# Squares of the weights' bound set behind other work with an output tile of their own, and preparation and folds put on 24 steps, in an attention-and-FFN kernel

## The chip, the cores and the metric

The kernel runs on one core of one Trainium2 chip. The time is the device time of one execution in microseconds; the median of three runs stands for a kernel. The engines that matter are TensorE (PE, with its weight loads as PEld), VectorE (DVE), ScalarE (ACT), GpSimd (POOL), and the DMA queues of SyncE (SP).

## The reference

Inputs are q, k, v of shape (8, 8, 576, 64), phi of shape (8, 8, 576, 32), and the float64 weights w_in (512 x 2048) and w_out (2048 x 512). For each batch and head, 32 memory slots are formed from 576 positions, and the queries attend to the slots; the heads side by side are the 512 model columns of 4608 tokens.

```python
a = phi - np.max(phi, axis=2, keepdims=True)          # over the 576 positions
a = np.exp(a)
a = a / (np.sum(a, axis=2, keepdims=True) + 1e-09)
k_m = np.einsum('bhsm,bhsd->bhmd', a, k)
v_m = np.einsum('bhsm,bhsd->bhmd', a, v)
scores = scale * np.matmul(q, k_m.transpose(0, 1, 3, 2))
scores = scores - np.max(scores, axis=-1, keepdims=True)
attn = np.exp(scores)
attn = attn / (np.sum(attn, axis=-1, keepdims=True) + 1e-09)
x = np.matmul(attn, v_m)      # then transposed and reshaped to 4608 x 512
h = x @ w_in
g = h * np.cos(h)
out = g @ w_out
```

## The kernel before, in words

The values of the slots are never applied to the queries alone. For each batch b, `fold` multiplies the 32 slot values of every head (`vm`) with w_in, so that the attention weights `aT` (256 of them per token: 8 heads by 32 slots) meet a folded matrix `vw` of 256 x 2048. The first product of a token group is then h = aT · vw, and the second is g · w_out.

**Groups and steps.** The 4608 tokens are 12 groups of 384, d_ff is 16 chunks `f` of 128; the main loop runs over i = 0 to 191, a step being one chunk of one group. In a step `gemm1` makes `hp` (128 x 384) in one of three PSUM buffers, `act` and `act_end` make g from it, and `gemm2` adds it into three accumulators of 128 x 512, four steps later (`LAG`). The chain of a step is: hp on TensorE, rounding on ACT (L544, tile `gp`), a subtraction on DVE (L547, tile `u`), Sin on ACT (L552), the product with hp on DVE (L554 in group 0, L556 later), which gives the PSUM buffer of hp back, and, from group 1 on, the split of g in two f16 parts (ACT L558, DVE L559). `hp_0_7` below is group 0, chunk 7.

**Group 0** runs in f32 with two matmuls for hp (L524) and three for the accumulators (L572), because the f16 parts of the weights are not there yet. During it the raw float64 weights arrive by DMA, in eight pieces `raw_in` of w_in and eight `raw_out` of w_out; `to_float32` turns one piece into f32 with two DVE operations (L143, L152) and two on ACT (L147, L151), and a third operation on ACT, L154, sums the squares of the piece (Square with `accum_out`) into a column of `sq`. Its elementwise result isn't needed and goes into the low words of the raw tile, over the input that has been read; the raw buffer therefore comes free when the square is done. `weight_scale` takes the largest of the sums as a bound of the weights, from which the scales of the f16 parts follow. `convert_next` takes one piece in each step (steps 0 to 13); `fold_first` makes the folded matrix of batch 0 in f32 for a piece of w_in (L495, then the copy `vf`, L497, on ACT for the first two pieces, on an engine that the scheduler takes for the others).

**Groups 1 to 11** run with split f16: 6 or 12 matmuls for hp (L533) and 9 for the accumulators (L577). In group 1, `w_out_split`, `w_in_split` and `split_first` make the f16 parts.

**Preparation of a batch** (`prep`: `memory`, then `attend`) is a generator whose pieces the main loop takes one after the other among its steps: the maximum of phi over positions, subtraction and exponential (L260), the products `psA` (L270), the normalised `X`, its transpose `tpx` (L292), the bound of the values (`l1` to `ev`), the scores `sc` (L376) brought to SBUF with a DVE transpose (L381), their softmax (L444), and the way back into `aT`. The list `jobs` gives each batch a first and last step, and 24 pieces are dealt out over 10 to 18 steps, so that several fall into one step. The folds of a batch (four, of 512 columns: matmuls, then a split on ACT, L477, and on DVE, L478) come every fourth step, the first `before - 1` steps ahead of use: 12 steps for even batches from 4 on, 4 or 5 for the others (counted from the step in which the batch is first used). psA, tpx, sc, the folds and the broadcast of the maximum share two PSUM buffers (`ps_s`).

**The maximum.** Batches 0 to 3: DVE reduces a transposed copy phiT that the host lays out (batch 0: TensorE transposes instead), and TensorE spreads the result over the partitions (L245, tile `top`). Batches 4 to 7: `maximum` reduces over partitions on POOL (L223).

**Order.** Each engine runs its own queue in order. A scheduler takes the instructions by priority, the order in which the program issues them, and by what is ready in its model; `keep_in_program_order` ties an instruction to the one before it on its engine. So where a piece is issued in the program sets roughly, not exactly, where it stands in a queue. ACT must load a table of functions when Exp follows Sin or the other way round (`ACT_TABLE_LOAD`).

Of the kernel before, what the change touches and what calls it, by code (L numbers as in the profile page):

```python
# [44 lines left out]
@with_exitstack
def attention_then_ffn(ctx: ExitStack, tc: tile.TileContext, phi, phiT, kv, qT, w_in, w_out, eye, out):
# [84 lines left out]

    sq = const.tile([P, 2, NW], F32, name="sq")

    def to_float32(dst, raw, sq_to, pin=False, after_sign=None):
# [19 lines left out]
        nc.scalar.activation(low.bitcast(F32), dst, AF.Square, accum_out=sq_to)  # L154
# [62 lines left out]
    def maximum(b):  # L217
        a = loads["phi", b]
        mx = ld.tile([P, 3, HM], F32, tag="phiT", name=f"mx_{b}", bufs=1)
        nc.vector.tensor_tensor(out=mx[:, 0:2], in0=a[:, 0:2], in1=a[:, 2:4], op=ALU.max)  # L220
# [1 line left out]
        nc.vector.tensor_tensor(out=mx[0:S - 512, 0], in0=mx[0:S - 512, 0], in1=a[0:S - 512, 4], op=ALU.max)
        nc.gpsimd.partition_all_reduce(mx[:, 2], mx[:, 0], channels=P, reduce_op=RED.max)  # L223
# [3 lines left out]
    def memory(b):  # L227
        a = loads.pop(("phi", b))
        if b == 0:

            mx = ld.tile([P, 2, HM], F32, tag="phiT", name="mx_first", bufs=1)
            nc.vector.tensor_tensor(out=mx, in0=a[:, 0:2], in1=a[:, 2:4], op=ALU.max)
            nc.vector.tensor_tensor(out=mx[:, 0], in0=mx[:, 0], in1=mx[:, 1], op=ALU.max)
            nc.vector.tensor_tensor(out=mx[0:S - 512, 0], in0=mx[0:S - 512, 0], in1=a[0:S - 512, 4], op=ALU.max)
# [4 lines left out]
        if b < NT:

            nmx = wk.tile([P, 2], F32, tag="nmx", name=f"nmx_{b}", bufs=1)
            nc.vector.tensor_reduce(out=nmx, in_=loads.pop(("phiT", b)) if b else mt[:, 0:2], op=ALU.max, axis=AX.X)
            top = small_ps(f"top_{b}")[:, 0:HM]
# [552 lines left out]
```

## Time and profile before

| | us |
|---|---|
| median of three runs (lowest, highest) | 710.82 (710.67, 712.17) |
| the profiled execution's own time | 710.08 |
| its span | 708.3 |
| TensorE busy | 687.8 (97%) |
| VectorE busy | 532.7 (75%) |
| ScalarE busy | 518.7 (73%) |
| mean granted clock of TensorE | 0.994 |

The trace is of one execution; its span is shorter than its time by what lies around it. A row of the timeline has start, length, engine, line, operation, output and input tile, count, and in brackets how long the engine had been idle before and on what it waited. A row of the groups has busy time, mean nanoseconds of one, and the idle time ahead of it with what ended most of that. A row of the waits has the total, how often, and the longest. Consecutive matmuls overlap, so the busy time of a group is less than its count times the mean.

### The profile page before, as it was taken

The page shows a single profiled execution, that of the slowest core. Times are in us where ns is not written, and L with a number is a line of the kernel's source. Part 1 is how long each engine was busy: PE and PEld are TensorE (multiplying, and loading weights), DVE is VectorE, ACT ScalarE, POOL GpSimd, SP SyncE. Part 2 cuts the span into 40 slices and gives each one's busy share as a digit, 9 for nine tenths or more (in the row PEclk, how much of TensorE's full clock was granted, in tenths as well). Part 3 has the DMA queues.
Part 4 walks back from the last instruction along what each step waited for, and adds up shares of the span by engine and source line. Part 5 has one row for each costly group of instructions (what it writes and reads, how often), then busy time and mean ns, then how long its engine had stood idle before and what let it go on. Part 6 is the DMA issues. An engine that isn't in the chain of part 4 may idle for free.

```text
span 708.3 us, 11822 instructions
## 1 busy us (share of the span) xinstructions
PE 687.8 (97%) x4597; PEld 364.7 (51%) x4597; DVE 532.7 (75%) x1135; ACT 518.7 (73%) x951; POOL 13.7 (2%) x34
## 2 busy tenths in 40 slices
PE   8699899999999999999999999999999999999997
PEld 3354345565555445666445445666445454665553
DVE  3889879999968966599667886599567976575552
ACT  1899999897985865778666875778766875665652
POOL 0000000000000000000000100000000000000000
PEclk9999999999999999999999999999999999999999
DMA  8996782326407100160105200160100000100101
GB/s 281 379 321 218 266 293 60 105 61 195 146 1 237 44 1 1 56 226 1 44 1 167 99 16 1 46 206 31 44 2 2 22 23 1 46 1 1 45 1 44
DMA packets 31959, 66.18 MB, mean 93 GB/s; under 512 B 2208, under 2 KB 12320, under 8 KB 31904
## 3 DMA queue, kind: packets, MB, share of 16 engines
q1 hardware_dynamic: 27440, 57.43, 25.0%
q10 hardware_dynamic: 4464, 8.00, 3.0%
q8 instruction: 36, 0.59, 0.3%
q14 instruction: 19, 0.16, 0.1%
HBM read 51.79 MB, written 9.44 MB: 86 GB/s over the span
## 4 chain that ended last, share of the span: by engine, by line
PE 60%; DVE 21%; ACT 16%; DMA 2%; issue 1%; ACTq 0%; POOL 0%; DVEq 0%; SPq 0%
PE acc L577 33%; PE hp L533 16%; DVE u L547 4%; ACT u L552 3%; DVE u L556 3%; DVE gp L559 3%; PE psA L270 3%; DVE vw L478 2%; PE sc L376 2%; PE pv L471 2%; ACT gp L558 2%; DMA phi<-in_phi 2%; DVE wo L191 2%; PE hp L524 1%; DVE w_in_parts L202 1%
## 5 line engine op out<-in xcount | busy, mean ns | idle before, releaser
L577 PE MATMUL acc<-wo,gp 128*128 128x512 f16 x1584 | 371.8, 379 | 1.2 <-DVE ob L589 0.7
L577 PEld LDWEIGHTS <-gp 128*128 128x128 f16 x1584 | 153.3, 98 | 162.6 <-issue 4.1
L533 PE MATMUL hp<-aT,vw 128*128 128x192 f16 (+1 forms) x1440 | 202.7, 284 | 1.0 <-DVE u L556 1.0
L533 PEld LDWEIGHTS <-vw 128*128 128x128 f16 x1440 | 128.3, 98 | 77.4 <-issue 17.5
L552 ACT ACTIVATE u<-u,quarter 128x384 f32<-128x384 f32 x192 | 116.7, 615 | 63.8 <-DVE u L547 62.9
L556 DVE SCALAR_TENSOR_TENSOR u<-hp,u 128x384 f32<-128x384 f32 x176 | 96.5, 553 | 60.6 <-ACT u L552 60.1
L544 ACT ACTIVATE gp<-hp,cu 128x192 int32<-128x192 f32 (+1 forms) x240 | 115.4, 492 | 28.1 <-PE hp L533 12.3
L547 DVE SCALAR_TENSOR_TENSOR u<-hp,cu,gp 128x192 f32<-128x192 f32 (+1 forms) x240 | 118.8, 503 | 21.9 <-ACT gp L544 21.5
L559 DVE TENSOR_TENSOR gp<-u,gp 128x384 f16<-128x384 f32 x176 | 96.4, 552 | 43.0 <-ACT gp L558 41.9
L558 ACT CAST gp<-u 128x384 f16<-128x384 f32 x176 | 88.8, 510 | 54.3 <-DVE u L556 53.0
L572 PE MATMUL acc<-wo,gp 128*128 128x512 f32 x96 | 45.1, 599 | 0.0
L478 DVE SCALAR_TENSOR_TENSOR vw<-pv,vw 128x512 f16<-128x512 f32 x48 | 31.5, 684 | 3.0 <-ACT vw L477 2.9
L524 PE MATMUL hp<-aT,vf 128*128 128x384 f32 x64 | 25.6, 533 | 7.9 <-DVE vf L497 3.1
L477 ACT ACTIVATE vw<-pv 128x512 f16<-128x512 f32 x48 | 26.8, 589 | 1.1 <-PE pv L471 0.9
L572 PEld LDWEIGHTS acc<-wo,gp 128*128 128x128 f32 x96 | 17.4, 190 | 17.8 <-issue 15.2
L601 ACT ACTIVATE ob<-acc,os 128x512 f32<-128x512 f32 x27 | 17.8, 682 | 9.6 <-PE acc L577 7.1
L524 PEld LDWEIGHTS hp<-aT,vf 128*128 128x128 f32 x64 | 12.2, 202 | 20.1 <-issue 4.3
L552 ACT ACT_TABLE_LOAD x17 | 21.8, 1283 | 0.3
L270 PE MATMUL psA<-kv,phi 128*32 128x129 f32 (+1 forms) x640 | 21.0, 275 | 0.7 <-ACT phi L260 0.5
L376 PE MATMUL sc<-q,km 128*64 128x256 f32 (+3 forms) x192 | 19.8, 342 | 1.6 <-DVE vw L478 1.2
L270 PEld LDWEIGHTS psA<-kv,phi 128*32 128x32 f32 (+1 forms) x640 | 16.4, 109 | 7.3 <-issue 3.3
L376 PEld LDWEIGHTS sc<-q,km 128*64 128x64 f32 x192 | 12.1, 140 | 12.0 <-issue 3.6
(136 smaller groups left out, 544.7 us busy)
## 6 DMA issues: line engine op xcount, KB each, us to landing
kv<-in_kv SPq DMA_DIRECT2D x32, 516.0 KB, 6.9
raw_out<-in_w_out SPq DMA_DIRECT2D x8, 1024.0 KB, 5.8
q<-in_qT SPq DMA_DIRECT2D x7, 1152.0 KB, 6.0
out<-ob ACTq DMA_DIRECT2D x30, 256.0 KB, 2.1
raw_in<-in_w_in SPq DMA_DIRECT2D x6, 1024.0 KB, 8.1
phi<-in_phi SPq DMA_DIRECT2D x8, 512.0 KB, 5.9
w_in_sb<-w_in_parts SPq DMA_DIRECT2D x12, 256.0 KB, 4.0
kv<-in_kv SPq DMA_DIRECT2D x8, 258.0 KB, 8.5
```

The costliest lines, as they stand in the source:

```text
L270: nc.tensor.matmul(psA[32 * j:32 * (j + 1), g * KV:(g + 1) * KV], lhsT=a[:n, c, h * M:(h + 1) * M], rhs=kvs[c][:n, h * KV:(h + 1) * KV], s ...
L376: nc.tensor.matmul(sc[D * p:D * (p + 1), g * n:(g + 1) * n], lhsT=km[:, 2 * g + p], rhs=qt[:, 2 * g + p, t0:t0 + n], start=True, stop=True)
L478: nc.vector.scalar_tensor_tensor(out=vw[:, 1, g], in0=src, scalar=T, in1=vw[:, 0, g], op0=ALU.mult, op1=ALU.subtract)
L533: nc.tensor.matmul(hp[:, c0:c0 + n], lhsT=vw[:, wi, g, fo * P:(fo + 1) * P], rhs=aT[:, ai, g, c1:c1 + n], start=(k == 0), stop=(k == 5))
L544: ins = nc.scalar.activation(ni[:, c], hp[:, c], AF.Copy, scale=cu, bias=0.25)
L547: nc.vector.scalar_tensor_tensor(out=u[:, c], in0=hp[:, c], scalar=cu, in1=ni[:, c], op0=ALU.mult, op1=ALU.subtract)
L552: nc.scalar.activation(u, u, AF.Sin, scale=TWO_PI_BELOW, bias=quarter)
L556: nc.vector.scalar_tensor_tensor(out=u, in0=hp[:, :GT], scalar=2.0 ** -17, in1=u, op0=ALU.mult, op1=ALU.mult)
L558: nc.scalar.copy(gp[:, 0], u)
L559: nc.vector.tensor_tensor(out=gp[:, 1], in0=u, in1=gp[:, 0], op=ALU.subtract)
L572: nc.tensor.matmul(accs[grp][t], lhsT=gp[:, t * P:(t + 1) * P], rhs=wo[:, f + 1], start=(f == 0), stop=(f == NF - 1))
L577: nc.tensor.matmul(accs[grp][t], lhsT=gp[:, gi, t * P:(t + 1) * P], rhs=parts[:, wi], start=(f == 0 and gi == 0 and wi == 0), stop=(f == N ...
```

## The change

Six things change. (1) L154, the square, is no longer issued where the piece is converted: it is put into a list, and from step 2 on up to two of the list are issued at the end of a step; what is left goes out before `weight_scale`. Its output is an f16 tile of its own, `sink`, written contiguously, which takes a place called "mx"; the raw buffer comes free with the DVE operation before it. (2) `phiT` with its three loads, its reduction and the broadcast matmuls are gone for batches 1 to 3; these use `maximum` as the later ones do. Batch 0 keeps its way. (3) The transpose of X is a transpose instead of a product with the identity in f32. (4) `part` ties the matmuls of one piece (psA, scores, folds) to one another. (5) Pieces go by a plan: one piece per step, 16 of them, from seven steps ahead of psA (`maximum`) and three (subtraction, exponential) to thirteen behind. psA of an even batch stands 30 steps before use, of an odd one 22 (batch 2: 24). Folds start eight steps behind psA, four steps apart; `scales` one step before the first of them. Batch 1 has a plan of its own (steps 1 to 8), and its folds stay at 12, 16, 20 and 24. (6) The copies `vf` from the third piece on are fixed to DVE.

```diff
+PLAN_FIRST = [1, 2, 2, 3, 3, 4, 4, 4, 5, 5, 6, 6, 7, 7, 8, 8]
+PLAN = [-7, -3, 0, 1, 2, 3, 4, 5, 6, 7, 8, 9, 10, 11, 12, 13]
...
+    def part(piece, *args, **kw):
+        ins = nc.tensor.matmul(*args, **kw)
+        if piece_of[0] == piece:
+            tc.keep_in_program_order(ins)
+        piece_of[0] = piece
...
-        if 0 < b < NT:
-            loads["phiT", b] = t = ld.tile([P, 2, S], F32, tag="phiT", name=f"phiT_{b}", bufs=1)
-            nc.sync.dma_start(out=t, in_=phiT[b].rearrange("(g p) s -> p g s", p=P))
...
-        nc.scalar.activation(low.bitcast(F32), dst, AF.Square, accum_out=sq_to)
+        squares.append(lambda: nc.scalar.activation(
+            st["sink"].rearrange("p (c x) -> p c x", c=dst.shape[1]), dst, AF.Square, accum_out=sq_to))
...
     def weight_scale(kind, name):
+        while squares:
+            squares.pop(0)()
...
-            nc.tensor.matmul(tpx[:, g * P:(g + 1) * P], lhsT=X[:, g], rhs=ident, start=True, stop=True)
+            nc.tensor.transpose(tpx[:, g * P:(g + 1) * P], X[:, g], ident)
...
-        (nc.scalar.copy if j < 2 else nc.any.tensor_copy)(out=st["vf", q][:, :, r * WS:(r + 1) * WS], in_=pv)
+        (nc.scalar.copy if j < 2 else nc.vector.tensor_copy)(out=st["vf", q][:, :, r * WS:(r + 1) * WS], in_=pv)
...
-        before, length = {1: (5, 10), 2: (5, 13), 3: (6, 16)}.get(b, (6, 17) if b % 2 else (13, 18))
-        jobs.append((b, use - before - length, use - before - 1))
+        if b == 1:
+            plan, first_fold = PLAN_FIRST, 12
+        else:
+            p0 = use - (22 if b % 2 else 30) + 6 * (b == 2)
+            plan, first_fold = [p0 + x for x in PLAN], p0 + (8 if b % 2 else 8)
+        at_step.setdefault(plan[0], []).append((b, True))
+        for x in plan[1:]:
+            at_step.setdefault(x, []).append((b, False))
         for q in range(NQ):
-            folds.setdefault(use - before + 4 * q + 1, []).append((b, q))
+            folds.setdefault(first_fold + 4 * q, []).append((b, q))
...
+        if i > 1:
+            if squares and "sink" not in st:
+                st["sink"] = ld.tile([P, NP * WS], F16, tag="mx", name="sink", bufs=1)
+            for _ in squares[:2]:
+                squares.pop(0)()
```

How the queues change is seen in the order of the instructions. First ACT at the start of group 0, before the change; the squares are the rows of L154, with the raw tile as their output:

```order
L151 ACTIVATE raw_out_0_111<-raw_out_0_111 128x1024
L544 ACTIVATE gp_0_0_337<-hp_0_0_333 128x384
L147 ACTIVATE w_in_sb_86<-wo_87 128x4x256
L154 ACTIVATE raw_in_1_108,sq_90<-w_in_sb_86 128x1024
L497 COPY vf_0_268<-pvf_1_297 128x2x256
L154 ACTIVATE raw_out_0_111,sq_90<-wo_87 128x1024
L552 ACT_TABLE_LOAD
L552 ACTIVATE u_0_0_336<-u_0_0_336,quarter_84 128x384
```

The same stretch after the change, where lines have moved by a few (the conversions are now L154 and L158, the square L161, the rounding L547, Sin L555):

```order
L158 ACTIVATE raw_out_0_111<-raw_out_0_111 128x1024
L547 ACTIVATE gp_0_0_332<-hp_0_0_328 128x384
L154 ACTIVATE w_in_sb_86<-wo_87 128x4x256
L547 ACTIVATE gp_0_1_371<-hp_0_1_367 128x384
L500 COPY vf_0_267<-pvf_1_295 128x2x256
L555 ACT_TABLE_LOAD
L555 ACTIVATE u_0_0_331<-u_0_0_331,quarter_84 128x384
L158 ACTIVATE wo_87<-wo_87 128x1024
L555 ACTIVATE u_0_1_370<-u_0_1_370,quarter_84 128x384
```

Two squares and a copy of vf stood ahead of the first sine; now the second rounding and the copy do, and the first square stands behind step 2's sine, some eleven rows further on.

Second, ACT between the sines of steps 6 and 7 of group 0, before:

```order
L552 ACTIVATE u_0_6_592<-u_0_6_592,quarter_84 128x384
L154 ACTIVATE raw_in_5_347,sq_90<-w_in_sb_86 128x1024
L411 ACTIVATE aT_1_497<-back_1_0_605 128x2x256
L147 ACTIVATE wo_87<-raw_out_3_396 128x1024
L151 ACTIVATE raw_out_3_396<-raw_out_3_396 128x1024
L552 ACTIVATE u_0_7_620<-u_0_7_620,quarter_84 128x384
```

and after the change (`at_1` is the softmax of batch 1):

```order
L555 ACTIVATE u_0_6_585<-u_0_6_585,quarter_84 128x384
L447 ACT_TABLE_LOAD
L447 ACTIVATE at_1_516<-at_1_516 128x640
L161 ACTIVATE sink_447,sq_90<-w_in_sb_86 128x1024
L154 ACTIVATE wo_87<-raw_out_3_385 128x1024
L158 ACTIVATE raw_out_3_385<-raw_out_3_385 128x1024
L547 ACTIVATE gp_0_7_611<-hp_0_7_607 128x384
L414 ACTIVATE aT_1_515<-back_1_0_622 128x2x256
L154 ACTIVATE wo_87<-raw_out_4_454 128x1024
L161 ACTIVATE sink_447,sq_90<-wo_87 128x1024
L555 ACT_TABLE_LOAD
L555 ACTIVATE u_0_7_610<-u_0_7_610,quarter_84 128x384
```

An exponential with two table loads around it, another conversion and a second square have moved between the two sines; the rounding gp_0_7 stands there too, which before came ahead of u_0_6.

Third, DVE in the scores of batch 5, in group 6 before the change (`vw_4_3` is the last fold of batch 4; `sc_5` its neighbour's scores):

```order
L394 TENSOR_REDUCE rs_5_4018<-at_5_4016 128x16
L559 TENSOR_TENSOR gp_6_0_4039<-u_6_0_4038,gp_6_0_4039 128x384
L478 SCALAR_TENSOR_TENSOR vw_4_3_4055<-pv_4_3_0_4056,vw_4_3_4055 128x512
L478 SCALAR_TENSOR_TENSOR vw_4_3_4055<-pv_4_3_1_4065,vw_4_3_4055 128x512
L381 STREAM_TRANSPOSE at_5_4016<-sc_5_512_4078 128x128
L547 SCALAR_TENSOR_TENSOR u_6_1_4095<-hp_6_1_4088,cu_4_3585,gp_6_1_4096 128x384
```

and at the same pieces of batch 5 after it, now in group 5:

```order
L384 STREAM_TRANSPOSE at_5_4010<-sc_5_0_4013 128x512
L562 TENSOR_TENSOR gp_5_14_3993<-u_5_14_3992,gp_5_14_3993 128x384
L384 STREAM_TRANSPOSE at_5_4010<-sc_5_256_4018 128x512
L392 TENSOR_REDUCE rm_5_4011<-at_5_4010 128x16
L393 TENSOR_TENSOR at_5_4010<-at_5_4010,rm_5_4011 128x512
L550 SCALAR_TENSOR_TENSOR u_5_15_4032<-hp_5_15_4025,cu_3_2294,gp_5_15_4033 128x384
L384 STREAM_TRANSPOSE at_5_4010<-sc_5_512_4049 128x128
```

The fold of batch 4 stood ahead of the last piece of the scores; no row of `vw_4` is left there, and `vw_4_3` stands some 50 rows earlier.

More of the change, by code (lines that the diff above doesn't have):

```diff
@@ L130, in load_w_out @@
         loads["out", j] = t
+    squares = []
     sq = const.tile([P, 2, NW], F32, name="sq")
@@ L227, in memory @@
     def memory(b):
+        if b == 0:
+            maximum(0)
         a = loads.pop(("phi", b))
         if b == 0:
[L231 to L234, printed above, removed]
             mt = small_ps("mx_T").rearrange("p (g x) -> p g x", x=P)
             for g in range(2):
-                nc.tensor.transpose(mt[:, g], mx[:, 0, g * P:(g + 1) * P], ident)
+                nc.tensor.transpose(mt[:, g], st["mx", 0][:, g * P:(g + 1) * P], ident)
             yield
[L239 to L243, printed above, removed]
+            nmx = wk.tile([P, 2], F32, tag="nmx", name="nmx", bufs=1)
+            nc.vector.tensor_reduce(out=nmx, in_=mt[:, 0:2], op=ALU.max, axis=AX.X)
+            top = small_ps("top")[:, 0:HM]
             for g in range(2):
@@ L256, in memory @@
                                           op=ALU.subtract)
[L257 removed]
+            if b > 1:
                 tc.keep_in_program_order(ins)
@@ L732, in attention_then_ffn @@
         for b, q in folds.get(i, ()):
+            fold(b, q)
+        for b, q in folds.get(i + 1, ()):
             if q == 0:
                 scales(b)
-            fold(b, q)
         if i % 48 in (8, 24) and i > 8:
             out_scales(2 * (i // 48) + (i % 48 == 24))
-        for b, s, e in jobs:
-            if i == e - 6 and NT <= b + 1 < B:
-                maximum(b + 1)
-            s = max(s, 0)
-            if s <= i <= e:
-                if b not in gens:
-                    gens[b] = [prep(b), 0]
-                want = math.ceil((i - s + 1) * NSTEP / (e - s + 1))
-                while gens[b][0] is not None and gens[b][1] < want:
-                    gens[b][1] += 1
-                    if next(gens[b][0], "end") == "end":
-                        gens[b][0] = None
-                if i == e:
-                    for _ in gens[b][0] or ():
-                        pass
+        for b, top in at_step.get(i, ()):
+            if top:
+                maximum(b)
+                gens[b] = prep(b)
+            else:
+                next(gens[b])
+        if i > 1:
[3 more added lines that the diff above has]
+                squares.pop(0)()
         if i in (11 * NF + 4, 11 * NF + 6):
@@ L758, in attention_then_ffn @@
         gemm2(*p)
-_INS = ["phi", "phiT", "kv", "qT", "w_in", "w_out", "eye"]
+_INS = ["phi", "kv", "qT", "w_in", "w_out", "eye"]
 def kernel(**inputs):
@@ L776 @@
         "phi": np.ascontiguousarray(phi.transpose(0, 2, 1, 3)).reshape(B, S, HM),
-        "phiT": np.ascontiguousarray(phi[:NT].transpose(0, 1, 3, 2)).reshape(NT, HM, S),
         "kv": kv.reshape(B, S, H * KV),
```

30 lines of the change are left out of this document (13 added, 17 removed).

## The prediction

> **What bounds the kernel now.** I read the shares of the engines first, then the chain that ended last.
>
> ```profile
> span 708.3 us, 11822 instructions
> PE 687.8 (97%) x4597; PEld 364.7 (51%) x4597; DVE 532.7 (75%) x1135; ACT 518.7 (73%) x951; POOL 13.7 (2%) x34
> PE 60%; DVE 21%; ACT 16%; DMA 2%; issue 1%; ACTq 0%; POOL 0%; DVEq 0%; SPq 0%
> ```
>
> TensorE is busy for 97% of the span, and 37% of the chain still runs over VectorE and ScalarE. An average hides where that is, so the next view is the busy time in stretches (sum, then PE, weight loads, DVE, ACT and POOL with counts, granted clock, DMA).
>
> ```profile
> 20.00:40.00 20.00, 13.03 (x55) 6.12 (x55) 15.98 (x24) 18.49 (x24) 0.00 (x0) 0.95 1.05 367
> 60.00:80.00 20.00, 16.86 (x56) 7.88 (x56) 18.35 (x33) 17.93 (x24) 0.31 (x1) 0.91 0.78 270
> 120.00:140.00 20.00, 19.27 (x125) 11.13 (x124) 19.89 (x42) 17.91 (x37) 0.00 (x0) 1.00 0.35 93
> 640.00:660.00 20.00, 20.00 (x117) 10.85 (x115) 11.34 (x24) 11.55 (x24) 0.00 (x0) 1.00 0.00 1
> ```
>
> There are two stages. Near the end (last row) TensorE is full and ACT and DVE are little over half busy: there only removed matmuls, or removed gaps in them, are worth time. In group 0 (20 to about 108 us) ACT is at 18 of 20, and TensorE has gaps: 7 us idle before 40, 3.1 us between 60 and 80 with the granted clock at 0.91. There the order on ACT and DVE decides, and in group 1 too, where DVE is at 19.9. The waits of TensorE name the gaps (total, times, longest); the first three rows are for 27 to 110 us, the rest for 110 to 708, rows of PEld being its weight loads.
>
> ```profile
> PE hp L524 <- DVE vf L497: 3.1, 1, 3.1
> PE hp L524 <- DVE gp L554: 2.1, 1, 2.1
> PE hp L524 <- DVE aT L406: 0.9, 1, 0.9
> ...
> PE sc L376 <- DVE vw L478: 1.2, 1, 1.2
> ...
> PEld sc L376 <- DVE vw L478: 2.1, 2, 1.7
> PEld psA L270 <- ACT phi L260: 1.4, 2, 1.0
> PEld psA L270 <- DVE vw L478: 1.3, 3, 0.5
> ```
>
> **The change part by part.** *Removed matmuls.* The broadcast of the maximum (L245) goes for batches 1 to 3, and the transpose of X (L292) issues two records a batch where there were four.
>
> ```profile
> 42.57 0.61 PE L245 MATMUL top<-ident,nmx 128*128 128x128 f32 x4
> L245 PE MATMUL top<-ident,nmx 128*128 128x128 f32 x16 | 2.7, 281 | 0.1
> L292 PE MATMUL tpx<-ident,X 128*128 128x128 f32 x32 | 5.8, 283 | 0.2 <-DVE X L287 0.2
> ```
>
> Four records take 0.61 us, one alone 0.28: the three others add 0.33, so a record costs 0.11 us in the stream. Batches 2 and 3 lose four each: 2 × 0.45 = 0.9 us. Batches 2 to 7 lose two each in L292: 6 × 0.22 = 1.3 us. Batch 1's six lie in group 0, where TensorE waits anyway, so I count them at nothing; without that cover they are worth another 0.7. Batch 0's L292 lies in the startup chain (0.2, left out). Sum: −2.2 us.
>
> *The maximum of batches 1 to 3* moves from one DVE reduction to three DVE operations and one on POOL:
>
> ```profile
> L242 DVE TENSOR_REDUCE nmx<-phiT 128x2 f32<-128x1152 f32 x3 | 4.0, 1338 | 0.0
> L220 DVE TENSOR_TENSOR mx<-phi 128x512 f32<-128x512 f32 x4 | 2.7, 686 | 1.5 <-DMA phi<-in_phi 1.5
> L223 POOL PARTITION_ALL_REDUCE mx<-mx x4 | 5.1, 1278 | 22.9 <-DVE mx L222 11.8 <-DVE rs L395 11.1
> ```
>
> One reduction is 1.34 us; the largest of the new three is 0.69, the other two handle half that width or less, so DVE's sum stays about level, and POOL's 1.28 us have four steps in which to finish. Nothing, in DVE's slack; for batch 1, in group 0, at most the 1.3 us of POOL if the subtraction is next on DVE. Three loads of phiT leave SP's queue ahead of phi and kv, where the transfers between 20 and 40 us run at a share of 1.05 of the engines. They come earlier, and a raw buffer is now free once the last DVE operation of a conversion has read it; but the first conversions wait for DVE and ACT as well; I take nothing, with 2 us of gain as the other end.
>
> *Squares and table loads on ACT.* The sixteen squares stay; each is issued up to two per step behind the step's work and writes contiguous f16.
>
> ```profile
> L154 ACT ACTIVATE raw_out<-wo 128x1024 f32<-128x1024 f32 x8 | 9.3, 1161 | 0.0
> L260 ACT ACTIVATE phi<-phi 128x1024 f32<-128x1024 f32 x7 | 7.4, 1058 | 0.1
> L552 ACT ACT_TABLE_LOAD x17 | 21.8, 1283 | 0.3
> L497 ACT COPY vf<-pvf 128x512 f32<-128x512 f32 x4 | 2.3, 574 | 0.0
> ```
>
> The trace has no contiguous f16 square; between the strided 1.16 and the contiguous 1.06 of L260 I take 1.06, 16 × 0.1 = −1.6, the other end being nothing. The order has 34 table loads before and 44 after, two of the ten in group 0: +2.6 there. Two of the four copies of vf go from ACT to DVE: −1.1 there, as much more on DVE. ACT's sum over group 0 is therefore level, and what counts is the order. The eight others fall into steps where ACT is little over half busy: nothing, since it idles 8.4 us of the 20 from 640 on and its two table loads around an exponential are 2.6; without that cover they cost up to 2.6 a batch.
>
> ```profile
> 34.20 1.28 ACT L552 ACT_TABLE_LOAD   x1
> 35.50 0.61 ACT L552 ACTIVATE u<-u,quarter 128x384 f32<-128x384 f32 x1
> ```
>
> Here the sine starts 0.02 us after its 1.28 us load. The Trainium skill (ScalarE: Activation LUTs, What ACT_TABLE_LOAD costs) gives a switch 1.28 us and a drain of 1.38 besides, about 2.66 in all, which speaks against this change; the trace shows no such drain ahead of the sine. By the page the two loads in group 0 would cost 5.3 us, an estimate, and that would leave the sum 2.7 higher.
>
> *Group 0, by hand.* Two places matter. First, in the order before, hp_8 waits for a copy of vf on DVE:
>
> ```profile
> 71.02 0.62 ACT L552 ACTIVATE u<-u,quarter 128x384 f32<-128x384 f32 x1
> 71.54 1.15 ACT L154 ACTIVATE raw_in<-w_in_sb 128x1024 f32<-128x1024 f32 x1
> 72.65 0.63 ACT L411 ACTIVATE aT<-back 128x512 f16<-128x512 f32 x1
> 73.17 1.35 ACT L147 ACTIVATE wo<-raw_out 128x1024 int16<-128x1024 uint8 x1
> 74.37 1.11 ACT L151 ACTIVATE raw_out<-raw_out 128x1024 f32<-128x1024 f32 x1
> 75.37 0.62 ACT L552 ACTIVATE u<-u,quarter 128x384 f32<-128x384 f32 x1
> 60.63 1.56 PE L524 MATMUL hp<-aT,vf 128*128 128x384 f32 x4
> 75.52 4.54 PE L524 MATMUL hp<-aT,vf 128*128 128x384 f32 x8 [3.14 <-DVE vf L497]
> 105.67 1.40 DVE L478 SCALAR_TENSOR_TENSOR vw<-vf,T,vw 128x512 f16<-128x512 f32 x2
> 107.87 1.15 PE L533 MATMUL hp<-aT,vw 128*128 128x192 f16 x12
> ```
>
> The wait is 3.14 us, and the eight matmuls behind it take 4.54 where twice 1.56 = 3.1 is normal: 1.4 more, together 4.5. In the new order that copy is no longer behind it, so I let this gap go. The Trainium skill (TensorE: Matmul & The Clock Gate, Part 1) has the clock fall to half after an idle window and return after some 3.4 us; the 4.54 and the 0.91 agree, and by it any new gap of that length costs about 1.4 on top.
>
> Second, a gap of that kind comes up elsewhere. Between the sines of steps 6 and 7 ACT now holds a table load, an exponential, two squares, two of L147, one of L151, gp_7, aT and another table load. From the rows: 2 × 1.28 + 2 × 1.06 + 2 × 1.35 + 1.11 + 0.63, then 0.5 for gp_7 and 0.7 for the exponential (384 and 640 elements beside aT's 512) and 0.62 for the sine, is about 10.9 us, against 75.37 − 71.02 = 4.4 before. The product on hp_7 behind that sine gives back the buffer that hp_10 needs; behind hp_10 on TensorE stand the matmuls of acc, whose gp wait for the same sine. Of the 6.5 us more, TensorE still has about 1.1 us of queued work, one and a half hp at 1.56 / 2; I take 5.4 as lost. Against 4.5 won that gives +0.9. Two squares of 1.15 stood ahead of the first sine and now none do; of these 2.3 us I let 0.4 last to the end of the group. Group 0: +0.5 (−1.5 to +4). Before, the last split of vf on DVE ends at 107.07, 0.8 ahead of the first f16 hp, and that piece keeps its place in the order; but group 1, where ACT and DVE are near full, now takes batch 2's first pieces with a table load of 1.28 more: +1. Groups 0 and 1: **+1.5**, between −6 (both gaps closed) and +6 (the new gap runs at half clock, and nothing is won in the first).
>
> *Spread preparation and folds.* In the steady part, the stalls were the small PSUM buffers of a fold standing between the pieces of one preparation:
>
> ```profile
> 394.99 1.28 DVE L478 SCALAR_TENSOR_TENSOR vw<-pv,vw 128x512 f16<-128x512 f32 x2
> 395.73 0.45 PE L376 MATMUL sc<-q,km 128*64 128x64 f32 x8 [1.23 <-DVE vw L478]
> ```
>
> The order puts the last fold of an even batch some eight steps ahead of the next batch's scores, and the exponentials of phi three steps ahead of psA; so these rows go. How much is there: TensorE's own waits from 110 us on sum to 3.8 us, those of its weight loads to 7.4 more, parts of which are hidden behind a running matmul; 4 to 11 us therefore. Some come back where folds of odd batches (now from step 14 before use) share the two buffers with the next piece. I take **−5**, near the lower end, with 0 and −10 as bounds.
>
> Sum against the profiled execution's own 710.08 us: −2.2 − 5 + 1.5 = −5.7, 704.4. That execution lies 0.74 under the median of the runs, 710.82, so on the median's footing 705.1; with the 0.2 at startup, **704.9 us**.
>
> **The rivals.** (A) *The steady gain comes, group 0 gets worse* by 5.5 instead of 1.5: 708.9. The 10.9 us in front of one sine speak for it; against it, that ACT's sum is level and TensorE has work to catch up with. (B) *The other side: ACT's queue in group 0 sets the end.* If two more sines stand behind table loads and squares as step 7's does, TensorE waits twice over 3 us and runs at half clock behind each (2 × 4.5 = 9): 704.9 + 9 = 713.9. It decides from the point where the first f16 hp, now at 107.87, comes later than about 116 (107.87 + 0.5 + the 7.3 that lie between 704.9 and 712.2). Against it: ACT had 1.5 to 2 us to spare in the windows of 20 to 80. (C) *The stalls only move*: the ten table loads and folds of odd batches make as many new ones, the −5 is nothing: 709.9. For it: the two small buffers stay two, and a batch's pieces and the folds of its neighbour still share them; against it: both named releasers are gone from those places. (D) *Both gaps close*: stalls −8 and groups 0 and 1 at −2.5: 704.9 − 3 − 4 = 697.9. For it: the upper bound of the stalls is 11; against it, the wait for hp_10. That the change does not do what it says is no rival: the order shows the squares behind the conversions.
>
> **How the numbers follow.** The forecast, with its own range 701.5 to 707.5, has 0.50, A 0.15, B 0.12, C 0.13, D 0.10. A measurement of this kernel can tell about 0.2% from no change, 1.4 us: faster is below 709.4. Faster: forecast, A and D, 0.75; the same: C, 0.13; slower: B, 0.12. The range from 698 to 712.5 leaves out B and half of D, 0.17.
>
> **What would show it.** The first f16 hp (107.87 now) between 106 and 112; the PE wait for vf L497 gone and one of 4 to 6 us for a gp of step 7 or near it in its place, with PEclk below 1 there; no wait of sc for vw behind 110 us, and PE and weight-load waits there under half of 3.8 and 7.4; 20 fewer PE records in steady preparation (8 of L245, 12 of L292). I am wrong if group 0 moves by more than 4 us, or if the steady part keeps its stalls.

## The result and the profile after

The changed kernel takes 723.25 us (719.1 to 724.15) beside 710.96 of the kernel before: 1.6% slower, a ratio of 1.0158 with an interval of 1.0117 to 1.0200. The forecast was 704.9 with a range up to 712.5; it is wrong in sign and in size. First the page of the profile after:

```profile
span 721.8 us, 11777 instructions
PE 689.4 (96%) x4569; PEld 362.2 (50%) x4569; DVE 537.2 (74%) x1142; ACT 528.8 (73%) x960; POOL 19.0 (3%) x37
PE 52%; ACT 20%; DVE 18%; DMA 7%; issue 2%; SPq 0%; POOL 0%; ACTq 0%; DVEq 0%
```

TensorE has 28 matmuls fewer than before and is busy for 1.6 us more, in a span that is 13.5 us longer. Its share of the chain fell from 60 to 52%; transfers rose from 2 to 7%. DVE and ACT grew by 4.5 and 10.1 us. The waits of TensorE (total, times, longest), from 27 to 112 us (first two rows) and from 112 on:

```profile
PE acc L575 <- DVE wo L159: 5.3, 2, 3.0
PE hp L527 <- DVE gp L557: 3.7, 3, 1.5
...
PE hp L536 <- DVE u L559: 9.2, 5, 3.3
PE tpx L295 <- DVE vw L481: 1.4, 1, 1.4
```

The wait for vf on DVE (3.1 before) is gone, and so are TensorE's own rows of sc and psA; tpx waits 1.4 for a fold. In their place hp waits for DVE in the main chain of a step, 9.2 us where it was 1.0. TensorE's own waits behind 112 us sum to 11.3 us and those of its weight loads to 10.2, where the prediction wanted less than half of 3.8 and 7.4. The timeline has the places (start, length, engine, line, what, idle ahead):

```profile
54.45 2.08 PE L575 MATMUL acc<-wo,gp 128*128 128x512 f32 x2 [2.26 <-DVE wo L159]
63.38 2.74 PE L575 MATMUL acc<-wo,gp 128*128 128x512 f32 x6
79.74 2.84 PE L575 MATMUL acc<-wo,gp 128*128 128x512 f32 x6 [3.00 <-DVE wo L159]
84.04 1.56 PE L527 MATMUL hp<-aT,vf 128*128 128x384 f32 x4 [1.45 <-DVE gp L557]
111.69 0.49 PE L536 MATMUL hp<-aT,vw 128*128 128x192 f16 x4
139.59 3.79 PE L536 MATMUL hp<-aT,vw 128*128 128x192 f16 x24 [2.09 <-DVE u L559]
184.72 2.08 PE L536 MATMUL hp<-aT,vw 128*128 128x384 f16 x6 [3.32 <-DVE u L559]
313.73 2.00 PE L536 MATMUL hp<-aT,vw 128*128 128x192 f16 x12 [2.39 <-DVE u L559]
476.33 1.15 PE L536 MATMUL hp<-aT,vw 128*128 128x192 f16 x12 [1.10 <-DVE u L559]
```

Twelve matmuls of hp take 2.00 us behind the gap at 313 and 1.15 behind the shorter one at 476. The windows view has a granted clock of 0.50 behind the first, so a gap can be paid twice, as waiting and as half clock:

```profile
313.90:317.20 3.30, 3.30 (x16) 2.15 (x15) 3.03 (x8) 2.98 (x9) 0.05 (x1) 0.50 0.03 7
```

To see in which stage the time went, the span of every profiled execution is cut at the first hp, at the first f16 hp (end of group 0), and at the first accumulator matmul of groups 3 and 11, all taken from the start times of TensorE's matmuls. The column of groups 1 and 2 begins at the first f16 hp; group 11 and the end, 44.8 to 44.9 us in every kernel, are left out. The table holds the experiments told below too.

| kernel | to first hp | group 0 | groups 1, 2 | groups 3 to 10 | table loads | median us |
|---|---|---|---|---|---|---|
| before | 27.0 | 80.9 | 130.5 | 425.0 | 34 | 709.74 to 710.96 |
| changed | 27.7 | 84.0 | 141.8 | 423.4 | 44 | 723.25 |
| e1 squares in place | 27.2 | 83.2 | 138.7 | 422.3 | 46 | 718.97 |
| e2 parts issued by POOL | 27.3 | 84.4 | 146.4 | 422.0 | 44 | 729.12 |
| e3 maximum tied | 26.6 | 82.6 | 135.4 | 419.6 | 44 | 712.27 |
| e4 e1 + e2 + e3 | 26.8 | 83.4 | 143.5 | 419.6 | 46 | 719.06 |
| e5 e3 + e1 | 27.7 | 83.3 | 136.2 | 419.6 | 46 | 713.68 |
| e7 e3 + all exponentials tied | 27.0 | 79.9 | 139.9 | 421.8 | 30 | 713.61 |
| e9 e7 + e1 | 26.5 | 80.1 | 141.0 | 421.8 | 32 | 718.00 |
| e10 e3 + batch 1's exponentials tied | 27.3 | 80.5 | 136.5 | 419.6 | 42 | 710.31 |
| e11 tied for batches 4 to 7 | 27.4 | 83.4 | 140.8 | 419.6 | 44 | 715.63 |
| e12 tied for batches 2, 3 | 27.0 | 82.5 | 136.2 | 424.2 | 44 | 716.58 |
| e13 e3 + old steps | 27.3 | 82.5 | 131.1 | 423.4 | 40 | 711.43 |
| e16 e13 + batch 1's exponentials tied | 26.8 | 80.7 | 130.8 | 423.3 | 38 | 708.98 |
| e6 before + squares deferred | 27.1 | 82.5 | 130.5 | 424.8 | 36 | 712.45 |
| e14 e6 + batch 1's exponentials tied | 27.6 | 83.7 | 129.5 | 424.6 | 34 | 712.64 |
| e15 e14 + transpose of X | 26.7 | 83.7 | 129.0 | 426.2 | 34 | 712.22 |
| e17 before + transpose of X | 29.3 | 82.8 | 129.2 | 424.8 | 34 | 712.00 |

Of the 13.5 us, 3.1 lie in group 0, 11.3 in groups 1 and 2, 0.7 ahead of the first hp, and groups 3 to 10 win 1.6. The plan moves 48 more fold matmuls than before (three folds, at 0.98 us each) out of groups 3 to 10 into groups 1 and 2. Without those 2.9 us, groups 1 and 2 lose 8.4 and groups 3 to 10 lose 1.3. Executions of one kernel differ by more than single cells do (the changed kernel's go from 719.1 to 724.15), while groups 3 to 10 agree within 0.1 in five kernels (419.6). I therefore take it that differences of 1 us in the first three columns carry nothing; with one trace for each kernel that isn't shown.

How much of the two later columns is idle time of TensorE shows in the windows view (length first, then TensorE's busy time; the granted clock is the third number from the end). The rows are groups 1 and 2 and groups 3 to 10, before, in the changed kernel and in e3:

```profile
107.87:238.42 130.55, 129.23 (x912) 70.85 (x910) 121.39 (x267) 108.78 (x206) 3.03 (x7) 1.00 0.37 109
238.42:663.43 425.01, 422.31 (x3000) 228.81 (x2999) 307.86 (x663) 300.52 (x582) 7.33 (x13) 1.00 0.13 45
111.69:253.50 141.81, 134.46 (x942) 71.09 (x942) 125.52 (x276) 118.95 (x220) 7.66 (x10) 0.98 0.37 102
253.50:676.91 423.41, 419.29 (x2944) 227.35 (x2942) 306.76 (x655) 299.27 (x576) 6.18 (x12) 1.00 0.13 45
109.13:244.49 135.36, 131.61 (x944) 69.64 (x944) 124.42 (x275) 119.29 (x222) 7.67 (x9) 1.00 0.37 107
244.49:664.08 419.59, 417.65 (x2945) 226.43 (x2942) 307.76 (x658) 299.79 (x576) 7.27 (x13) 1.00 0.13 45
```

Before the change TensorE idled for 1.3 us in groups 1 and 2 and for 2.7 us in groups 3 to 10. After it, it idles for 7.4 and 4.1.

### The profile page after: what moved, and what is told of

The parts are those of the page before. It is cut to its first block, busy times and chain, and to the rows that moved or that the text cites. A ratio compares the mean times of both kernels' runs of the same rounds, so it can differ in the third digit from the quotient of the medians.

```text
span 721.8 us, 11777 instructions
## 1 busy us (share of the span) xinstructions
PE 689.4 (96%) x4569; PEld 362.2 (50%) x4569; DVE 537.2 (74%) x1142; ACT 528.8 (73%) x960; POOL 19.0 (3%) x37
## 4 chain that ended last, share of the span: by engine, by line
PE 52%; ACT 20%; DVE 18%; DMA 7%; issue 2%; SPq 0%; POOL 0%; ACTq 0%; DVEq 0%
PE acc L580 31%; PE hp L536 16%; ACT u L555 4%; DVE u L550 3%; DMA phi<-in_phi 3%; DVE u L559 3%; DVE gp L562 3%; ACT gp L561 3%; PE pv L63 2%; DVE vw L481 2%; ACT gp L547 2%; DMA w_in_sb<-w_in_parts 2%; PE sc L63 2%; ACT sink L161 1%; DMA kv<-in_kv 1%
## 5 line engine op out<-in xcount | busy, mean ns | idle before, releaser
L536 PE MATMUL hp<-aT,vw 128*128 128x192 f16 (+1 forms) x1440 | 205.0, 287 | 9.4 <-DVE u L559 9.2
L536 PEld LDWEIGHTS <-vw 128*128 128x128 f16 x1440 | 129.9, 99 | 86.3 <-issue 28.2
L555 ACT ACTIVATE u<-u,quarter 128x384 f32<-128x384 f32 x192 | 115.6, 613 | 61.0 <-DVE u L550 60.3
L547 ACT ACTIVATE gp<-hp,cu 128x192 int32<-128x192 f32 (+1 forms) x240 | 114.0, 489 | 33.7 <-PE hp L536 16.3
L527 PE MATMUL hp<-aT,vf 128*128 128x384 f32 x64 | 24.0, 500 | 5.6 <-DVE gp L557 3.7
L604 ACT ACTIVATE ob<-acc,os 128x512 f32<-128x512 f32 x27 | 17.9, 684 | 13.3 <-PE acc L580 11.3
```

The source lines that it names most:

```text
L527: nc.tensor.matmul(hp[:, :GT], lhsT=st["vf", q][:, g, fo * P:(fo + 1) * P], rhs=st["aTf"][:, g], start=(g == 0), stop=(g == 1))
L536: nc.tensor.matmul(hp[:, c0:c0 + n], lhsT=vw[:, wi, g, fo * P:(fo + 1) * P], rhs=aT[:, ai, g, c1:c1 + n], start=(k == 0), stop=(k == 5))
L547: ins = nc.scalar.activation(ni[:, c], hp[:, c], AF.Copy, scale=cu, bias=0.25)
L555: nc.scalar.activation(u, u, AF.Sin, scale=TWO_PI_BELOW, bias=quarter)
```

## The experiments

**Three suspects, each undone alone: e1 to e4.** The trace of the changed kernel offered three causes. Squares stand ahead of conversions for which accumulator matmuls wait (54 and 79 us). The third block of w_in's f16 parts is issued late and lands later still, behind loads for batch 3 in SyncE's queue; first the issue rows of that queue, then ACT's wait for it:

```profile
136.36 1.25 SPq L223 DMA_DIRECT2D w_in_sb<-w_in_parts  x2
154.54 1.84 SPq L101 DMA_DIRECT2D kv<-in_kv  x2
156.52 0.38 SPq L93 DMA_DIRECT2D phi<-in_phi  x1
159.86 0.65 SPq L222 DMA_DIRECT2D w_in_sb<-w_in_parts  x1
```

```profile
175.70 1.33 ACT L211 ACTIVATE w_in_parts<-w_in_sb,s_in 128x512 f16<-128x512 f32 x2 [3.17 <-DMA w_in_sb<-w_in_parts]
```

And `maximum` waits for phi on DVE:

```profile
309.01 0.69 DVE L230 TENSOR_TENSOR mx<-phi 128x512 f32<-128x512 f32 x1 [2.85 <-DMA phi<-in_phi]
```

e1 issues the squares in place again:

```diff
-        squares.append(lambda: nc.scalar.activation(
-            st["sink"].rearrange("p (c x) -> p c x", c=dst.shape[1]), dst, AF.Square, accum_out=sq_to))
+        nc.scalar.activation(low.bitcast(F32), dst, AF.Square, accum_out=sq_to)
```

> The changed kernel with one part undone: each square is issued again right behind the conversion of its piece and writes the raw tile's low words; all else as changed (723.25 us, first f16 hp at 111.7). Theory: in group 0 the deferred squares stand ahead of later conversions on ScalarE, and TensorE waits for those (2.3 and 3.0 us for wo behind the DVE operation that ends a conversion); undone, the first f16 hp comes at about 108 and the time falls by 3 to 4, to 719.5. Rival (it is the ten extra table loads on ScalarE that cost the time, wherever they fall): the squares don't matter, 722 to 724.

Measured: 718.97 us, ratio to before 1.0116 (1.0074 to 1.0158). The size is the theory's, though with four runs each the intervals of e1 and of the changed kernel overlap. The place isn't: TensorE's waits for wo in group 0 fell from 5.3 to 2.1 us as expected, but group 0 stayed at 83.2, with two table loads more, and most of the gain lies in groups 1 and 2, whose order the edit changes as well. It doesn't show that the squares were the cause.

e2 issues the sixteen transfers of the parts from GpSimd:

```diff
-            nc.sync.dma_start(out=w2[here, :, o], in_=parts[here, 0])
-            nc.sync.dma_start(out=w2[there, :, o], in_=parts[here, 1])
+            nc.gpsimd.dma_start(out=w2[here, :, o], in_=parts[here, 0])
+            nc.gpsimd.dma_start(out=w2[there, :, o], in_=parts[here, 1])
```

> The changed kernel with the sixteen transfers of the w_in parts issued by GpSimd instead of SyncE, so that they no longer stand behind the loads of batch 3 in SyncE's queue (issue blocked from 136.4 to 154.5 us, third block at 159.9 instead of about 140). Theory: ScalarE's 3.2 us wait for that transfer at 175.7 and TensorE's 3.3 us at 184.7 with the half clock behind it go: 5 to 6 us less, 717.5 to 718. Rival (table loads): these waits only move to the next sine, 722 to 723.

Measured: 729.12, ratio 1.0269 (1.0240 to 1.0298), slower by 6 instead of faster by 5. GpSimd's queue, with nothing of batch 3 ahead of it, issued the third block at nearly the same time, and ACT's wait for it grew:

```profile
157.70 0.62 POOL L222 DMA_DIRECT2D w_in_sb<-w_in_parts  x1 [7.10 <-ACT vw L480]
```

```profile
172.93 0.72 ACT L211 ACTIVATE w_in_parts<-w_in_sb,s_in 128x512 f16<-128x512 f32 x1 [7.15 <-DMA w_in_sb<-w_in_parts]
```

In both kernels ACT (L211) finishes the last piece of that block only at 155.4 to 155.5 us, and GpSimd issues its transfer at 157.70, behind a split on ACT by the profile. The queue of SyncE, at 159.86, therefore held the block for 2.2 us at most. That suspect falls. The wait itself is on the path: in e2 ACT waits 7.15 us for the transfer, DVE 6.82 for ACT, and TensorE 5.74 for DVE, with a granted clock of 0.50 behind it:

```profile
176.25 0.70 PE L63 MATMUL sc<-q,km 128*64 128x64 f32 x8 [5.74 <-DVE at L384]
174.10:180.80 6.70, 4.55 (x25) 3.06 (x26) 6.38 (x15) 4.90 (x11) 0.31 (x1) 0.50 0.40 127
```

Why the transfer lands so late is not shown.

e3 ties the first DVE operation of `maximum` to its place:

```diff
-        nc.vector.tensor_tensor(out=mx[:, 0:2], in0=a[:, 0:2], in1=a[:, 2:4], op=ALU.max)
+        ins = nc.vector.tensor_tensor(out=mx[:, 0:2], in0=a[:, 0:2], in1=a[:, 2:4], op=ALU.max)
+        if b > 1:
+            tc.keep_in_program_order(ins)
```

> The changed kernel with the first DVE operation of the maximum of batches 2 to 7 tied to its place in the program, so that it no longer stands some 100 rows earlier on DVE, ahead of the landing of phi (DVE waits 2.85 us for that transfer at 309 us, TensorE 2.4 us, and again about 1.3 at 475). Theory: 2.4 and about 1 of half clock, and 1.3: 4 to 5 us less, 718.5 to 719. Rival (table loads): nothing, 722.5 to 724.

Measured: 712.27, ratio 1.0041 (1.0023 to 1.0059): 11 us of the 12.3 lost, more than twice what was expected. The order on DVE tells what the tie does. Of batch 5, the row of the maximum's first operation and of the subtraction that needs the result are, in the changed kernel and with the tie (number of the row on DVE in front):

```
changed  512 L230 TENSOR_TENSOR mx_5_3629<-phi_5_2959 128x512
changed  624 L259 TENSOR_TENSOR phi_5_2959<-phi_5_2959,mx_5_3629 128x1024
tied     610 L230 TENSOR_TENSOR mx_5_3629<-phi_5_2959 128x512
tied     625 L261 TENSOR_TENSOR phi_5_2959<-phi_5_2959,mx_5_3629 128x1024
```

The plan puts the maximum in step 83; the scheduler had moved it some hundred rows forward, presumably to where its model has phi_5 in place (the model is not on record). On the chip phi_5 had not landed, and everything on DVE behind it waited. The spread has its part in this: the load of phi_5 goes out when psA of batch 4 has read phi_4. In the kernel before (first four rows) psA stands 3.5 us behind the subtraction of batch 4, and DVE comes to the maximum of batch 5 at 17.1 us behind it. In the changed kernel (last three, with the row of 309.01 above as the fourth) psA stands 6.7 us behind it, and DVE is at the maximum already at 13.2 (309.01 less the wait of 2.85):

```profile
294.94 1.21 DVE L254 TENSOR_TENSOR phi<-phi,mx 128x1024 f32<-128x1024 f32 x1
298.40 2.54 PE L270 MATMUL psA<-kv,phi 128*32 128x129 f32 x80
301.05 0.38 SPq L87 DMA_DIRECT2D phi<-in_phi  x1
312.08 0.68 DVE L220 TENSOR_TENSOR mx<-phi 128x512 f32<-128x512 f32 x1
293.00 1.55 DVE L259 TENSOR_TENSOR phi<-phi,mx 128x1024 f32<-128x1024 f32 x2
299.68 2.54 PE L63 MATMUL psA<-kv,phi 128*32 128x129 f32 x80
302.55 0.38 SPq L93 DMA_DIRECT2D phi<-in_phi  x1
```

At batch 7 only psA has moved (from 4.3 to 6.7 us behind the subtraction), and DVE waits 1.56 us where it did not wait. DVE's waits for phi behind 200 us, all for batches 4 to 7, are, in the changed kernel and, below, in the kernel before:

```profile
DVE mx L230 <- DMA phi<-in_phi: 6.2, 4, 2.8
```

```profile
DVE mx L220 <- DMA phi<-in_phi: 1.5, 2, 1.0
```

With the tie there is no such row. Of the 12.9 us between the two profiled spans, groups 3 to 10 give 3.8, groups 1 and 2 give 6.4, group 0 and the startup 2.5. In groups 1 and 2 TensorE idles 3.6 us less and is busy for 2.9 less, its mean granted clock 1.00 in place of 0.98; in groups 3 to 10 it is 2.2 and 1.6.

e4 has the three edits together.

> All three edits together in the changed kernel. Theory: the three places are separate in time, so the gains add to 12 to 14: 709.5 to 711, at the time of before or a little under it. Rival (table loads): 720 or more.

Measured: 719.06, ratio 1.0132 (1.0110 to 1.0153). The gains don't add: groups 1 and 2 are at 143.5, with the loss of e2 in them.

**What is left after e3: e5, e6, e7, e9.** e5 is e3 with the diff of e1 on top.

> The maximum tied as in the run before (712.27 us), and the squares issued again right behind each conversion, into the raw tile. Theory S (what is left of the loss, group 0 taking 82.6 us from its first hp to the first f16 hp where it took 80.9, comes from the deferred squares standing ahead of conversions): group 0 back to 81, the time at 709.5 to 710.5. Theory T (it comes from the extra table loads on ScalarE): 712 to 713.

Measured: 713.68, ratio 1.0038 (1.0025 to 1.0050), with group 0 at 83.3: theory S's 81 didn't come, and theory T's time is missed by 0.7. With the maximum tied, squares in place win nothing; but two of the run's table loads are new and lie in group 0 (46 in all), so that S and T are not told apart. e6 defers the squares in the kernel before:

```diff
-        nc.scalar.activation(low.bitcast(F32), dst, AF.Square, accum_out=sq_to)
+        squares.append(lambda: nc.scalar.activation(
+            st["sink"].rearrange("p (c x) -> p c x", c=dst.shape[1]), dst, AF.Square, accum_out=sq_to))
...
+        if i > 1:
+            if squares and "sink" not in st:
+                st["sink"] = wk.tile([P, NP * WS], F16, tag="back", name="sink", bufs=4)
+            for _ in squares[:2]:
+                squares.pop(0)()
```

> The kernel before with one part of the change alone: the squares go into a list, up to two are issued behind a step from step 2, and write an f16 tile of their own, here one of the four buffers of the tiles back and ob. The parts that this leaves out (plan, maximum, transposes) are as before. Theory S: the deferral costs group 0 about 2 us, 712 to 714 beside 710 of before. Theory T: it moves work within a full ScalarE, and gains what the shorter contiguous writes save: 709 to 711.

Measured: 712.45, ratio 1.0033 (1.0021 to 1.0044): the deferral alone makes the kernel slower, by 1.6 us in group 0. It too brought two table loads with it (36), so that S and T were not told apart. The squares themselves are cheaper, as assumed (in the changed kernel 1.04 us against 1.15 to 1.16 before):

```profile
L161 ACT ACTIVATE sink<-wo 128x1024 f16<-128x1024 f32 x8 | 8.3, 1042 | 0.0
```

e7 ties the two exponentials of each softmax, on top of e3:

```diff
         for p in pieces:
-            nc.scalar.activation(piece(p)[0], piece(p)[0], AF.Exp)
+            tc.keep_in_program_order(nc.scalar.activation(piece(p)[0], piece(p)[0], AF.Exp))
```

> The maximum tied, and the two exponentials of a batch's softmax tied to their place in the program too, so that they follow each other on ScalarE: 30 table loads where the changed kernel has 44, two of the fourteen less in group 0 and some in group 1. Theory T: group 0 and 1, where ScalarE and VectorE are full, win 2.6 us each or a part of it, 708.5 to 710. Theory S: 712 to 713, since in the later groups ScalarE idles anyway.

Measured: 713.61, ratio 1.0054 (1.0037 to 1.0072). Group 0 falls by 2.7 us, close to two loads of 1.28, as theory T has it; but groups 1 and 2 rise by 4.5 and groups 3 to 10 by 2.2, with fourteen loads fewer. Outside group 0 fewer loads win nothing here. The tie, which holds exponentials back, may be what costs there; the two effects are not separated.

e9 is e7 with the diff of e1.

> The three edits together: maximum tied, exponentials tied, squares issued in place. Under S and under T alone it is at the better of the two runs above, 709 to 710; if both count, 706.5 to 708, faster than before by 0.3% or more.

Measured: 718.00, ratio 1.0115 (1.0079 to 1.0152), 4.4 slower than e7. The two profiled executions are nearly level (716.59 and 715.84), so the traces don't show the difference; what it is stays open. Putting the squares back in place thus gave −4.3, +1.4 and +4.4 us in three surroundings.

**Which ties, which stage: e10 to e13.** e10 ties, beside the maximum, the exponentials of batch 1 alone (the diff is against e7):

```diff
-            tc.keep_in_program_order(nc.scalar.activation(piece(p)[0], piece(p)[0], AF.Exp))
+            ins = nc.scalar.activation(piece(p)[0], piece(p)[0], AF.Exp)
+            if b == 1:
+                tc.keep_in_program_order(ins)
```

> The maximum tied (712.27 us), and the two exponentials of batch 1 alone tied to their place: two table loads fewer in group 0, where the run with all of them tied took 79.9 us instead of 82.6 from the first hp to the first f16 hp, but 3 us more in group 1. Theory T (the two table loads between the sines of steps 5 to 7 are what group 0 lost): group 0 at 80 again, group 1 near 62.5, the time 709 to 710, level with before or up to 0.3% faster. Rival O (every edit reorders group 1, where both engines are full, by as much as it wins): 711.5 to 714.

Measured: 710.31, ratio 1.0002 (0.9989 to 1.0016). Group 0 is at 80.5, 2.1 less for two loads less, and 1.1 comes back in groups 1 and 2. e11 and e12 take e3's tie for a part of the batches each:

```diff
-        if b > 1:
+        if b > 3:                # e11
+        if b in (2, 3):          # e12
             tc.keep_in_program_order(ins)
```

> The changed kernel with the maximum tied for batches 4 to 7 alone; batches 2 and 3 keep their early place. If each place pays for itself: groups 4 and 7 lose their waits for phi (57.2 to 53.9 and 54.5 to 53.9 us), and groups 1 and 2 keep theirs, 723.25 less 4 = 719. If the reordering that comes of the ties is what counts, groups 1 and 2 change too, and the time is anywhere from 712 to 723.

> The other half: the maximum tied for batches 2 and 3 alone. Groups 1 and 2 at 62.5 and 56.4 us instead of 67.9 and 58.3, the waits for phi in groups 4 and 7 stay: 723.25 less 7 = 716. If groups 1 and 2 stay at 67.9 and 58.3, the tie of these two is not what mended them.

Measured: 715.63, ratio 1.0090 (1.0066 to 1.0115), and 716.58, ratio 1.0096 (1.0071 to 1.0121). Each half acts on its own stage: e11 has groups 3 to 10 at the 419.6 of e3 and groups 1 and 2 near the changed kernel's, e12 the reverse. (The trace of e11 is of an execution of 718.34; what its median has less than that, 2.7, is not located.) In groups 1 and 2 it is not a wait for phi, though: for batches 2 and 3 none stands there, and the one for batch 4, 1.02 us at 226, is still there in e12 with 0.52. What the trace shows is ACT's order: in the changed kernel no sine is issued for 11.8 us, while pieces of splits, folds and output copies pass, and with the tie one comes after 6.8:

```profile
126.59 0.61 ACT L555 ACTIVATE u<-u,quarter 128x384 f32<-128x384 f32 x1
138.34 1.63 ACT L555 ACTIVATE u<-u,quarter 128x384 f32<-128x384 f32 x3
```

```profile
123.95 0.68 ACT L557 ACTIVATE u<-u,quarter 128x384 f32<-128x384 f32 x1
130.73 1.12 ACT L557 ACTIVATE u<-u,quarter 128x384 f32<-128x384 f32 x2
```

The gap of TensorE at 139.59 (2.09 us) stands behind the sine at 138.34, the one at 184.72 behind ACT's wait for the third block; behind both the granted clock is 0.50 (139.8 to 143.1 and 184.2 to 187.5 us). In e11 both are there too; in e3 and e12 the gaps are 1.1 to 1.3 us, and no half clock follows. Why an earlier maximum of batch 2 or 3 leads the scheduler to that order is not shown. e13 puts the pieces and folds of batches 2 to 7 back to the old steps, on top of e3:

```diff
-            p0 = use - (22 if b % 2 else 30) + 6 * (b == 2)
-            plan, first_fold = [p0 + x for x in PLAN], p0 + (8 if b % 2 else 8)
+            before, length = {2: (5, 13), 3: (6, 16)}.get(b, (6, 17) if b % 2 else (13, 18))
+            s = use - before - length
+            plan = [s - 4] + [s + k * (length - 1) // 14 for k in range(15)]
+            first_fold = use - before + 1
```

> The maximum tied, and the pieces and folds of batches 2 to 7 put back to the steps of the kernel before (several pieces in a step, folds 12 steps ahead of use for even batches and 4 or 5 for the others); batch 1, the squares and the transposes stay as changed. Theory P (the spread puts folds and pieces into groups 1 and 2, where VectorE is full, and wins nothing later): groups 1 and 2 fall from 118.9 us together to 114 or 115, the rest rises by the folds moved back and no more, 709.5 to 711. Rival (the spread does win stalls in groups 3 to 10): 714 or more.

Measured: 711.43, ratio 1.0021 (1.0008 to 1.0033), 0.8 under e3. Groups 1 and 2 fall by 4.3, of which the folds moved back are 2.9; groups 3 to 10 rise by 3.8. The spread therefore wins 0.9 late and loses 1.4 early: next to nothing.

**Closing the account: e14 to e17.** e14 is e6 with the exponentials of batch 1 tied, 34 loads as before.

> The kernel before with the squares deferred as in e6, and the two exponentials of batch 1 tied, so that it has 34 table loads again. If the table loads were the cost of the deferral: group 0 falls from 82.5 us to 80 or below, the time from 712.45 to 709.5 to 710.5, level with before or a little faster. If the deferral costs by itself: 712 to 713.

Measured: 712.64, ratio 1.0039 (1.0025 to 1.0053), group 0 at 83.7. So the deferral costs the old order time without more table loads; the tie, which moves the exponentials too, is in this run as well. TensorE's waits from 27 to 112 us name conversions that end late:

```profile
PE acc L578 <- DVE wo L153: 6.2, 2, 4.5
PE pvf L501 <- DVE w_in_sb L153: 3.6, 3, 2.4
```

That these come of the deferral is not shown: e6 has 1.6 us on wo in place of 6.2, and e17 below, with its squares in place, has 4.6.

e15 and e17 change the transpose of X alone, on e14 and on the kernel before:

```diff
-            nc.tensor.matmul(tpx[:, g * P:(g + 1) * P], lhsT=X[:, g], rhs=ident, start=True, stop=True)
+            nc.tensor.transpose(tpx[:, g * P:(g + 1) * P], X[:, g], ident)
```

> As e14, with X turned by a transpose of two records in place of four records of a product. By the rows, 0.22 us for each of batches 2 to 7 and 0.2 at the start: 1 to 1.5 less than e14. If the records were hidden: the same as e14.

> The kernel before with the transpose of X alone changed: by the rows 1.3 to 1.5 less, 708.8 to 709.2 beside 710.3. If the smaller model cost moves other instructions, up to 2 either way.

Measured: 712.22, ratio 1.0031 (1.0020 to 1.0042), 0.4 under e14; and 712.00, ratio 1.0030 (1.0017 to 1.0042), 2 us slower than before. Groups 3 to 10 are at 424.8 beside 425.0 in e17 and rise by 1.6 in e15: the 1.3 us of removed records don't show. Part of e17's loss in its profile is a late transfer at the start, whose wait ahead of psA the kernel before doesn't have, and a wait for a conversion in group 0, which is new too:

```profile
14.41 0.65 PE L270 MATMUL psA<-kv,phi 128*32 128x129 f32 x16 [1.04 <-DMA kv<-in_kv]
16.34 1.08 PE L270 MATMUL psA<-kv,phi 64*32 64x129 f32 x16 [0.74 <-DMA kv<-in_kv]
78.86 3.78 PE L572 MATMUL acc<-wo,gp 128*128 128x512 f32 x4 [4.60 <-DVE wo L152]
```

e16 is e13 with the exponentials of batch 1 tied.

> The changed kernel with the maximum tied, pieces and folds of batches 2 to 7 at the old steps (711.43 us) and the exponentials of batch 1 tied: if the 2 us that these won in group 0 add, 709 to 710; if the reordering takes them back, 711 to 713.

Measured: 708.98, ratio 0.9991 (0.9980 to 1.0001). Here the gains add (group 0 at 80.7, groups 1 and 2 at 130.8), and this is the best version; against the kernel before it is no measurable difference.

## Why the prediction was wrong, step by step

**The step that failed first** is the pricing of the maximum, in two terms. The sentence on batches 1 to 3, "Nothing, in DVE's slack; for batch 1, in group 0, at most the 1.3 us of POOL", priced the operations (0.69 and less, right) and not the place that the order gives them on DVE. With those of batches 2 and 3 tied (e12) groups 1 and 2 take 136.2 us in place of 141.8. That is 5.6 us, and it is no wait for a transfer but another order of the stage, whose reason stays open. The term of the spread counted the waits that go and put at nothing the one that it makes, for batches 4 to 7: the maximum ahead of the landing of phi, 6.2 us on DVE in place of 1.5. Tying those (e11) takes 3.8 us out of groups 3 to 10. In both places it was not asked where the order puts the first operation of the maximum. Both ties together give back 11 of 12.3 us (e3).

**Spread preparation and folds, −5.** Wrong by nearly all of it. The waits named did go, but with the maximum in order the spread wins 0.9 in groups 3 to 10 and pays 1.4 in groups 1 and 2 (e13 against e3). The size was out of reach as well: TensorE idled for 2.7 us in all of groups 3 to 10 and 1.3 in groups 1 and 2, so that most of the weight loads' 7.4 us in "4 to 11" ran beside matmuls.

**Groups 0 and 1, +1.5.** In group 0 half of the mechanism came: 10.9 us were forecast between the sines of steps 6 and 7, and the trace has 82.78 − 72.42 = 10.4. But the wait for the product behind that sine is 1.45 us (84.04) and not 5.4. The larger waits, 2.26 and 3.00 us on acc, are for conversions of wo on DVE, which the prediction put at nothing ("but the first conversions wait for DVE and ACT as well; I take nothing"). That the first f16 hp, at 111.69, lies inside the 106 to 112 named is therefore in part luck. The term was +0.5 and is +3.1. "ACT's sum over group 0 is therefore level" hides that the two table loads lie between sines. With the exponentials of batch 1 tied, and two loads fewer, group 0 takes 2.1 (e10), 1.8 (e16 beside e13) and 2.7 us less (e7), near the 2.6 of two loads; in the old order the same tie won nothing (e14, +1.2), so the loads alone are not shown to be the price.

```profile
72.42 0.62 ACT L555 ACTIVATE u<-u,quarter 128x384 f32<-128x384 f32 x1
73.05 1.28 ACT L447 ACT_TABLE_LOAD   x1
74.35 0.74 ACT L447 ACTIVATE at<-at 128x640 f32<-128x640 f32 x1
81.48 1.28 ACT L555 ACT_TABLE_LOAD   x1
82.78 0.61 ACT L555 ACTIVATE u<-u,quarter 128x384 f32<-128x384 f32 x1
```

That is 1.28 us a load, and the next function starts 0.02 us behind it. The Trainium skill (ScalarE: Activation LUTs, What ACT_TABLE_LOAD costs) would have 2.66 each, 5.3 for the two, an estimate; the rows don't show its drain. For group 1 the term was +1, from one more table load; it was +8.4 with group 2, and +2.0 with the maximum tied (e3). That the order of a stage where ACT and DVE are both nearly full could change as a whole was not among the rivals.

**Removed matmuls, −2.2.** Not seen: groups 3 to 10 with the maximum tied are 5.4 below before, 2.9 of it folds moved out, which leaves 2.5; but e17 shows that the transposes, 1.3 of the term, win nothing by themselves, so the agreement is no proof.

**The rivals.** B, the other side, gave 713.9 and was nearest, but by another mechanism and at another place: its own condition, a first f16 hp later than 116, didn't come true. C (the stalls only move) fits groups 3 to 10 in kind, but not with the table loads and folds that it named. Neither had DVE behind a transfer. The half clock behind a gap was as forecast (2.00 for twelve matmuls against 1.15); not every gap paid it, for six matmuls took 2.84 behind the 3.00 us at 79.74, against 2.74 without a gap. The Trainium skill (TensorE: Matmul & The Clock Gate, Part 1) has the clock fall after at least one idle window of about 3.4 us; here gaps of 2.09 and 2.39 us were enough.
